# Attention into a gated FFN on one core: tile 1 in two token halves, and the last numerators of batch 1 moved back

## The chip, the core and the metric

The kernel runs on one NeuronCore of a Trainium2 chip. TensorE multiplies matrices and writes to PSUM, VectorE and ScalarE compute elementwise and read PSUM, GpSimd issues most transfers and converts some tiles, SyncE issues DMA transposes. Each engine works through its own instructions strictly in order, and waits for the others through semaphores. The metric is the device time of one execution in microseconds (us); it is given as the median of several executions.

## The reference

Linear attention with a positional weighting (cosine and sine of the position), for 8 batches of 8 heads, 576 positions and 64 features, and then a feed-forward network on the 4608 tokens:

```python
def phi(x, c, s):
    r = np.maximum(x, 0.0)
    return np.concatenate([r * c, r * s], axis=-1)      # 64 -> 128 features
q_p = phi(q, cos_w, sin_w)
k_p = phi(k, cos_w, sin_w)
kv  = np.einsum('bhsf,bhsd->bhfd', k_p, v)              # 128 x 64 for each head
z   = np.sum(k_p, axis=2)
num = np.einsum('bhsf,bhfd->bhsd', q_p, kv)
den = np.einsum('bhsf,bhf->bhs', q_p, z)[..., None] + 1e-06
attn = num / den
x = attn.transpose(0, 2, 1, 3).reshape(B * S, H * D)    # 4608 x 512
a = x @ w1; b = x @ w2                                  # 512 -> 1024
h = a * b @ w3                                          # 1024 -> 1024
out = h @ w_out                                         # 1024 -> 512
```

Nothing stands between w3 and w_out, so the kernel multiplies these two once (w34 = w3 @ w_out) and then uses one matrix of 1024 x 512.

## The kernel before

The positions of a batch are cut into five chunks (four of 128 and one of 64). A chunk is loaded, turned into features ("kp", "qp"; the cosine half on VectorE, the sine half on ScalarE), its key side is summed into KV, and its query side, transposed, is multiplied by KV: the numerator, with the denominator in a 65th column. VectorE normalizes it into "xblk", and a transpose of that becomes part of "xT", an FFN tile of 512 tokens. There are nine such tiles, t = 0 to 8. Batch b begins at token 576 b, so tile 1 (tokens 512 to 1023) holds the remainder of batch 0 (chunk 4) and of batch 1 its chunks 4, 0, 1 and 2, in this order; chunk 3 is already in tile 2.

The FFN is a generator that yields after every group of matmuls. Yields are numbered through all tiles, and slot g holds what attention work is emitted after group g:

```python
    g = 0
    for t in range(NT):
        for _ in ffn_groups(t):
            for u in slots[g]:
                u()
            g += 1
```

Tile 0 has the groups 0 to 39: 16 of products, then 16 that make w34 (two for each block of w3), then 8 of the second FFN matmul. Tile 1 has the groups 40 to 63: 16 of products (40 to 55) and 8 of the second matmul. So a slot number is a place in the order of every engine. In tiles 0 and 1 the first four column blocks (jc 0 to 3, as two pairs) are made for the first 256 tokens and then for the second, the other four at once for all 512:

```python
        def multiply(a, b, pair, half):
            asb = fsb.tile([P, 512], BF16, name="asb")
            nc.scalar.copy(out=asb[:], in_=a[:, :])
            nc.vector.tensor_mul(out=abT[:, ts(pair, 2), ts(half, 256)],
                                 in0=asb[:].rearrange("p (i n) -> p i n", i=2),
                                 in1=b[:, :].rearrange("p (i n) -> p i n", i=2))

        def on_half(half):
            # ... (tile 0's finer cut left out)
            for pair in range(2):
                a, b = ffn_tile(), ffn_tile()
                # ...
                    for ps, w in ((a, w1b), (b, w2b)):
                        for i in range(2):
                            products(ps[:, ts(i, 256)], w, 2 * pair + i, ts(half, 256))
                        if w is w1b and (t == 1 or half == 0):
                            yield
                multiply(a, b, pair, half)
                yield

        if t < 2:
            yield from on_half(0)
            yield from on_half(1)
        for jc in range(4 if t < 2 else 0, 8):
            aT = ffn_tile()
            products(aT[:, :], w1b, jc, slice(0, 512))
            asb = fsb.tile([P, 512], BF16, name="asb")
            nc.scalar.copy(out=asb[:], in_=aT[:, :])
            yield
            bT = ffn_tile()
            products(bT[:, :], w2b, jc, slice(0, 512))
            nc.vector.tensor_mul(out=abT[:, jc, :], in0=asb[:], in1=bT[:, :])
            yield
```

"ffn_tile" goes round four PSUM banks. "num" makes a numerator: for batches 0 and 1 into the one two-bank PSUM buffer "pnum", or, with in_two, into two FFN banks that are normalized one by one. The same "pnum" takes KV (line 305) of each batch. "no_more_by_pe" ends TensorE's transposes through PSUM, and opens a second buffer for numerators in their place.

```python
    def num(b, c, chain=True, in_two=False):
        # ...
        banks = [ffn_tile(), ffn_tile()] if in_two else [nt[:, g, :] for g in range(2)]
        for h in range(H):                                            # line 365
            nc.tensor.matmul(banks[h // 4][:, ds((h % 4) * 65, 65)], lhsT=qpT[:, h, ds(at, 128)],
                             rhs=kvs[:, h, :], start=True, stop=True)
        # ... then on VectorE, for the whole or for each half:
                nc.vector.tensor_scalar_add(out=den[rows, g], in0=n4[:, :, :, 64], scalar1=1e-6)
                nc.vector.reciprocal(out=den[rows, g], in_=den[rows, g])
                nc.vector.tensor_tensor(out=xblk[rows, g], in0=n4[:, :, :, 0:D], ...)   # line 383

    def x_tr(b, c, by_vector=False):
        # ... batches from 2 on, and two chunks of 0 and 1: by a DMA transpose
        for kc in range(4):                                           # line 417
            nc.tensor.transpose(pst[:, kc, :], xf[:, ts(kc, 128)], identb[:])
        copy = nc.vector.tensor_copy if by_vector else nc.scalar.copy
        copy(out=xT[t][:, :, ds(o, R)], in_=pst[:, 0:4, rows])        # line 419
```

A chunk of queries is transposed by TensorE ("q_tr", eight transposes and one evacuation by VectorE) or, where "dma_q" names it, by a DMA transpose right after its features.

Of the kernel before, what the change touches and what calls it, by code (L numbers as in the profile page):

```python
# [68 lines left out]
def kernel(  # L69
# [11 lines left out]
    nc = tc.nc  # L81
# [54 lines left out]
    def load_first4(eng, t, src, b=0):  # L136
        eng.dma_start(out=t[0:64, :, 4, :], in_=src[b, :, 512:S, :].rearrange("h p d -> p h d"))
# [9 lines left out]
    def load_w3(jp, n):  # L147
        nc.gpsimd.dma_start(out=w3b[:, jp:jp + n, :],
                            in_=moe_w3[ds(jp * P, n * P), :].rearrange("(b p) l -> p b l", p=P))

    def load_wout(half):
        nc.gpsimd.dma_start(out=woutb[:, ts(half, 4), :],
                            in_=moe_w_out[ts(half, 512), :].rearrange("(c p) m -> p c m", p=P))
# [44 lines left out]

    load_w12(0, 256)
    load_w12(256, 256)  # L200
    load_first4(nc.gpsimd, q0, q)
    nc.gpsimd.dma_start(out=w1b[:, :, ds(512, 256)], in_=w1v[:, :, ds(512, 256)])

    def other_loads(behind):

        seen = sm.tile([P, 1], BF16, name="seen", bufs=1)
        nc.gpsimd.tensor_copy(out=seen[:], in_=behind)
        nc.gpsimd.dma_start(out=w2b[:, :, ds(512, 256)], in_=w2v[:, :, ds(512, 256)])
        load_w12(768, 256)
        for jp in range(2):  # L210
            load_w3(jp, 1)
            load_wout(jp)
        for jp in range(2, 4):
            load_w3(jp, 1)
        load_w3(4, 2)
        load(1, "k")
        load_w3(6, 2)
# [25 lines left out]
    def order_of(b):  # L243

        return [0, 1, 2, 3, 4] if b % 2 == 0 else [4, 0, 1, 2, 3]

    def dma_q(b):

        return order_of(b)[5 if b < 1 else 3 if b == 1 else 0:]

    feat = {}

# [203 lines left out]
    def ffn_groups(t):  # L456
        x = xT[t]
        abT = fsb.tile([P, 8, 512], BF16, name="abT", bufs=2)

        def products(out, w, jc, tok):  # L460
            for kc in range(4):
                nc.tensor.matmul(out, lhsT=w[:, kc, ts(jc, 128)], rhs=x[:, kc, tok],  # L462
                                 start=(kc == 0), stop=(kc == 3))
# [10 lines that stand above are left out]
            if half == 1 and t == 0:  # L474
                banks = [(ffn_tile(), ffn_tile()) for _ in range(2)]
                for quarter in range(2):
                    for pair, (a, b) in enumerate(banks):
                        for i in range(2):
                            for ps, w in ((a, w1b), (b, w2b)):
                                products(ps[:, ds(256 * i + 128 * quarter, 128)], w, 2 * pair + i,  # L480
                                         ds(256 + 128 * quarter, 128))
                        if quarter == 1:
                            multiply(a, b, pair, half)
                        if quarter == 0 or pair == 1:
                            yield
                return
            for pair in range(2):
                a, b = ffn_tile(), ffn_tile()
                if pair == 0 and t == 0:
                    for quarter in range(2):  # L490
                        for i in range(2):
                            for ps, w in ((a, w1b), (b, w2b)):
                                products(ps[:, ds(256 * i + 128 * quarter, 128)], w, i,
                                         ds(256 * half + 128 * quarter, 128))
                            if half == 0 and quarter == 0 and i == 0:
                                yield
                        if quarter == 0:
                            yield
                else:
# [8 lines that stand above are left out]
        if t < 2:  # L508
            yield from on_half(0)
            yield from on_half(1)  # L510
        for jc in range(4 if t < 2 else 0, 8):
            aT = ffn_tile()
            products(aT[:, :], w1b, jc, slice(0, 512))
            asb = fsb.tile([P, 512], BF16, name="asb")
# [6 lines that stand above are left out]
        if t == 0:  # L521
            for jp in range(8):
                for part in range(2):
                    w34_mm(jp, part)
                    yield
            early.close()
            holds.append(ctx.enter_context(tc.tile_pool(name="hold", bufs=HELD,
                                                        reuse_waits="tile")))
        for ms in range(3 if t == NT - 1 else 4):
            ops = ffn_tile()  # L530
            for jc in range(8):
                nc.tensor.matmul(ops[:, :], lhsT=abT[:, jc, ts(ms, 128)], rhs=w34b[:, jc, :],  # L532
                                 start=(jc == 0), stop=(jc == 7))
                if jc == 3:
                    yield
            if ms % 2 == 0:
                osb = holds[0].tile([P, 2, 512], FP32, name="osb")
                kept.append(osb)
            nc.scalar.copy(out=osb[:, ms % 2, :], in_=ops[:, :])  # L539
            if t == NT - 1:  # L540
                store(nc.sync, osb[:, ms % 2:ms % 2 + 1, :], 4 * t + ms, 1)
            yield
        if t == NT - 1:
            for half in range(2):
                cols = ts(half, 256)
                ops = ffn_tile()
                for jc in range(8):
                    nc.tensor.matmul(ops[:, 0:256], lhsT=abT[:, jc, ts(3, 128)],  # L548
                                     rhs=w34b[:, jc, cols], start=(jc == 0), stop=(jc == 7))
                nc.scalar.copy(out=osb[:, 1, cols], in_=ops[:, 0:256])  # L550
                store(nc.sync, osb[:, 1:2, :], 4 * t + 3, 1, cols)
                yield
# [6 lines left out]
    def at(s, *calls):  # L559
        slots[s] += calls  # L560
# [8 lines left out]
    def plan(b, kf, vc, kv, qf, nu, loads=None, xt=None):  # L569
        order = order_of(b)  # L570
        for i, c in enumerate(order):
            at(kf[i], lambda c=c: prep_k(b, c))
            at(qf[i], lambda c=c: prep_q(b, c))
            at(vc[i], lambda c=c: prep_v(b, c))
        for i, c in enumerate(order):
            at(kv[i], lambda c=c, i=i: kv_chunk(b, c, i))
        for i, c in enumerate(order):
            at(nu[i], lambda c=c: num(b, c, in_two=b == 1 and c in (0, 2)))
            at(xt[i] if xt else nu[i], lambda c=c: x_tr(b, c, by_vector=(b, c) == (1, 1)))

    def plan_loads(b, when):
# [38 lines left out]
    at(1, lambda: x_tr(0, 1, by_vector=True), lambda: q_tr(0, 3, evac=False)[1](), lambda: num(0, 2))  # L620
    at(3, lambda: x_tr(0, 2), lambda: num(0, 3))
    at(5, lambda: x_tr(0, 3))
    at(6, lambda: features(0, q0f, q0, 4))
    at(23, lambda: transpose_q(0, 4))
    at(7, lambda: load(1, "qv"), lambda: load(2, "q"))
    at(29, lambda: num(0, 4))
    at(11, lambda: feature_buffers(1))
    at(29, lambda: x_tr(0, 4))

    for jp, s in enumerate((13, 16, 18, 20, 22, 24, 26, 28)):  # L630
        at(s, lambda jp=jp: w3_tr(jp))

    plan(1, kf=(24, 25, 26, 27, 28), vc=(31, 31, 32, 32, 32), kv=(33, 33, 33, 34, 34),
         qf=(29, 30, 30, 31, 31), nu=(35, 36, 38, 39, 42), xt=(37, 38, 40, 42, 42))
    for c, s in zip(order_of(1), (31, 32, 34)):
        at(s, lambda c=c: q_tr(1, c))
    at(43, no_more_by_pe)
    plan_loads(2, (27, 28, 33, 35))
    plan(2, kf=(36, 37, 38, 40, 41), vc=(41, 42, 43, 44, 45), kv=(46, 46, 46, 47, 47),
         qf=(40, 41, 42, 43, 44), nu=(48, 50, 52, 54, 57))  # L640
    plan_loads(3, (36, 37, 47, 50, 54, 57))
    plan(3, kf=(54, 57, 59, 61, 63), vc=(64, 65, 66, 67, 68), kv=(71, 72, 72, 73, 73),
# [54 lines left out]
```

## Time and profile before

| what | before |
|---|---|
| median of 3 executions | 249.2 us (249.05 to 250.78) |
| profiled span | 246.9 us, 5034 instructions |
| TensorE, VectorE, ScalarE, GpSimd busy | 97%, 55%, 53%, 38% |
| products with w1 and w2 (line 462), share of the chain that ended last | 45% |
| second FFN matmul (line 532), the same | 24% |
| DMA, the same | 10% |

The page calls the engines PE, DVE, ACT and POOL; SP is SyncE. A line of the timeline gives the start and the duration of an instruction (or of a run of the same, "x4"), both in us, the engine, the line of the kernel, the operation, and output and input by the names in the program; in brackets, the idle time before it and what ended this. A busy time is the sum of durations; instructions of one engine overlap a little, so the distance of two starts is the better pace. The chain that ended last follows the execution back from its last instruction, at each step to what released it.

### The profile page before, as it was taken

Reading aid. Unit: us, or ns where it says so; the run is one execution under the profiler, and the core shown is the slowest. Engines: PE = TensorE matmul, PEld = TensorE weight load, DVE = VectorE, ACT = ScalarE, POOL = GpSimd, SP = SyncE. Lnnn points to the kernel's source line nnn. Section 1 sums busy time; section 2 is a strip of 40 time slices with the busy share of each in tenths; the row PEclk is TensorE's granted clock in tenths of the full one; section 3 lists DMA queues with packets and bytes.
Section 4 is the critical chain, followed back from the end, with each engine's and each line's share of the span. In section 5 each row is a group of like instructions: output and inputs, shape, how many; then the busy total and the mean of one; then the engine's idle time right before and its main releaser. Section 6 shows DMA issues by size and latency. Waiting matters only on the chain.

```text
span 246.9 us, 5034 instructions
## 1 busy us (share of the span) xinstructions
PE 240.5 (97%) x1872; PEld 130.4 (53%) x1872; DVE 135.9 (55%) x336; ACT 130.2 (53%) x266; POOL 93.4 (38%) x196
## 2 busy tenths in 40 slices
PE   8799999999999999999999999999999999999994
PEld 3479545566975445444544555454545554444443
DVE  7775652668968445647566475547464645312420
ACT  2676313767943873466556654854575333434332
POOL 7654342024512261127032612173322005978700
PEclk9999999999999999999999999999999999999999
DMA  7999999999999969999999999999994536998823
GB/s 199 178 194 199 201 207 204 198 181 173 153 162 142 167 100 149 132 149 134 169 144 155 118 180 150 150 140 140 166 142 89 94 64 214 260 281 289 282 101 128
DMA packets 86200, 41.22 MB, mean 167 GB/s; under 512 B 53792, under 2 KB 82720, under 8 KB 86176
## 3 DMA queue, kind: packets, MB, share of 16 engines
q0 software_dynamic: 37008, 27.20, 71.8%
q1 hardware_dynamic: 49168, 13.71, 35.9%
q8 instruction: 14, 0.23, 0.4%
q14 instruction: 10, 0.08, 0.1%
HBM read 38.80 MB, written 9.44 MB: 195 GB/s over the span
## 4 chain that ended last, share of the span: by engine, by line
PE 85%; DMA 10%; POOL 3%; issue 1%; ACT 0%; POOLq 0%
PE ffnps L462 45%; PE ffnps L532 24%; PE ffnps L237 6%; DMA woutb<-in_moe_w_out_dram 5%; DMA w2b<-in_moe_w_dram 5%; PE pnum L365 4%; PE pnum L305 4%; PE pst L225 1%; PE ffnps L548 1%; POOL qs L133 1%; POOL w1b L196 1%; PE pst L336 1%; POOL vs L133 0%; PE pst L417 0%; POOL w2b L197 0%
## 5 line engine op out<-in xcount | busy, mean ns | idle before, releaser
L462 PE MATMUL ffnps<-xT,w2b 128*128 128x512 bf16 (+2 forms) x344 | 75.5, 344 | 0.0
L462 PE MATMUL ffnps<-xT,w1b 128*128 128x512 bf16 (+2 forms) x344 | 75.5, 344 | 0.0
L519 DVE TENSOR_TENSOR abT<-asb,ffnps 128x512 bf16<-128x512 bf16 x64 | 43.9, 686 | 54.3 <-PE ffnps L462 52.4
L532 PE MATMUL ffnps<-w34b,abT 128*128 128x512 bf16 x280 | 65.0, 379 | 0.0
L515 ACT CAST asb<-ffnps 128x512 bf16<-128x512 f32 x64 | 37.4, 584 | 50.0 <-PE ffnps L462 45.2
L462 PEld LDWEIGHTS <-w2b 128*128 128x128 bf16 x344 | 31.0, 98 | 27.3
L462 PEld LDWEIGHTS <-w1b 128*128 128x128 bf16 x344 | 30.8, 98 | 25.9
L567 POOL COPY seen<-mark 1x1 bf16<-1x1 bf16 x50 | 8.9, 178 | 84.4 <-ACT mark L565 84.4
L532 PEld LDWEIGHTS <-abT 128*128 128x128 bf16 x280 | 26.0, 98 | 27.9 <-DVE abT L519 0.2
L539 ACT COPY osb<-ffnps 128x512 f32<-128x512 f32 x35 | 20.5, 584 | 35.2 <-PE ffnps L532 35.1
L274 ACT ACTIVATE qp<-qs,sinv 128x512 bf16<-128x512 bf16 (+2 forms) x40 | 28.1, 714 | 1.8 <-DMA qs<-in_q_dram 1.8
L383 DVE TENSOR_TENSOR xblk<-pnum,den 128x512 bf16<-128x512 f32 (+1 forms) x37 | 25.6, 691 | 1.3
L297 POOL COPY va<-vs 128x512 bf16<-128x512 bf16 (+1 forms) x30 | 17.6, 621 | 22.9 <-DMA vs<-in_v_dram 22.4
L274 ACT ACTIVATE kp<-ks,sinv 128x512 bf16<-128x512 bf16 (+1 forms) x35 | 25.0, 717 | 0.9 <-DMA ks<-in_k_dram 0.9
L447 POOL DMA_DIRECT2D out_dram<-osb x42 | 22.1, 531 | 2.7 <-issue 2.1
L365 PEld LDWEIGHTS <-qpT 128*128 128x128 bf16 x320 | 15.4, 98 | 8.7 <-DVE qpT L350 0.6
L381 DVE TENSOR_SCALAR den<-pnum 128x8 f32<-128x8 f32 (+1 forms) x37 | 6.0, 163 | 22.6 <-PE pnum L365 22.5
L237 PE MATMUL ffnps<-woutb,w3T 128*128 128x512 bf16 x64 | 15.8, 380 | 0.2 <-DMA woutb<-in_moe_w_out_dram 0.2
L365 PE MATMUL pnum<-kvs,qpT 128*128 128x65 bf16 x296 | 15.8, 194 | 0.0
L270 DVE TENSOR_SCALAR qp<-qs,cosv 128x512 bf16<-128x512 bf16 (+1 forms) x40 | 15.3, 389 | 0.7 <-DMA qs<-in_q_dram 0.7
L305 PEld LDWEIGHTS <-kp 128*128 128x128 bf16 x280 | 11.4, 98 | 4.1
L270 DVE TENSOR_SCALAR kp<-ks,cosv 128x512 bf16<-128x512 bf16 (+1 forms) x35 | 12.5, 367 | 0.0
(88 smaller groups left out, 181.6 us busy)
## 6 DMA issues: line engine op xcount, KB each, us to landing
out_dram<-osb POOLq DMA_DIRECT2D x16, 256.0 KB, 4.5
out_dram<-osb POOLq DMA_DIRECT2D x24, 128.0 KB, 3.9
qs<-in_q_dram POOLq DMA_DIRECT2D x8, 256.0 KB, 7.6
ks<-in_k_dram POOLq DMA_DIRECT2D x6, 320.0 KB, 6.3
qs<-in_q_dram POOLq DMA_DIRECT2D x6, 320.0 KB, 5.9
vs<-in_v_dram POOLq DMA_DIRECT2D x6, 320.0 KB, 5.7
ks<-in_k_dram POOLq DMA_DIRECT2D x6, 256.0 KB, 7.0
vs<-in_v_dram POOLq DMA_DIRECT2D x6, 256.0 KB, 5.4
```

The costliest lines, as they stand in the source:

```text
L237: nc.tensor.matmul(acc[:, :], lhsT=w3T[:, lc, :], rhs=woutb[:, lc, :], start=(lc == 0), stop=(lc == 7))
L270: nc.vector.tensor_scalar(out=dst[:R, c, :, 0:D], in0=src[:R, :, c, :], scalar1=0.0, scalar2=cosv[:R, at:at + 1], op0=ALU.max, op1=ALU.mult)
L274: nc.scalar.activation(out=dst[:R, c, 0:n, D:F], in_=src[:R, 0:n, c, :], func=ACTF.Relu, scale=sinv[:R, at:at + 1], bias=0.0)
L305: nc.tensor.matmul(kvt[:, h // 4, ds((h % 4) * 65, 65)], lhsT=kp[:, c, h, :], rhs=va[:, c, h, 0:D + 1], start=(i == 0 and h % 4 == 0), sto ...
L365: nc.tensor.matmul(banks[h // 4][:, ds((h % 4) * 65, 65)], lhsT=qpT[:, h, ds(at, 128)], rhs=kvs[:, h, :], start=True, stop=True)
L383: nc.vector.tensor_tensor(out=xblk[rows, g], in0=n4[:, :, :, 0:D], in1=den[rows, g].unsqueeze(3).to_broadcast([R, G, 4, D]), op=ALU.mult)
L447: eng.dma_start(out=rows[:, :, cols], in_=osb[64 * i:64 * i + rows.shape[0], :, cols])
L462: nc.tensor.matmul(out, lhsT=w[:, kc, ts(jc, 128)], rhs=x[:, kc, tok], start=(kc == 0), stop=(kc == 3))
L515: nc.scalar.copy(out=asb[:], in_=aT[:, :])
L519: nc.vector.tensor_mul(out=abT[:, jc, :], in0=asb[:], in1=bT[:, :])
L532: nc.tensor.matmul(ops[:, :], lhsT=abT[:, jc, ts(ms, 128)], rhs=w34b[:, jc, :], start=(jc == 0), stop=(jc == 7))
L539: nc.scalar.copy(out=osb[:, ms % 2, :], in_=ops[:, :])
```

## The change

It is a change of order, with one piece of work moved to another engine:

- Tile 1 is made in two token halves over all eight column blocks, 8 groups of 256 tokens and then 8 more, so that its second half of tokens is first needed at group 48 and not at 44.
- This gives room for the numerators of batch 1's chunks 1, 2 and 3: from slots 38, 39 and 42 to 41, 43 and 45. Chunk 2's is no longer made in two FFN banks, and the end of TensorE's transposes through PSUM moves from slot 43 to 46. Batch 2's key features move from 36-41 to 38-42.
- A third chunk of batch 1's queries (chunk 1) is transposed by DMA instead of TensorE.
- Both halves of w_out are loaded before the second block of w3, and the first transposes of w3 stand one slot earlier.
- The remainder of batch 0's queries (chunk 4, 64 KB) is loaded behind that block and no longer before most weights; its features move from slot 6 to 19.

```diff
--- before.py
+++ after.py
@@ -198,7 +198,6 @@
 
     load_w12(0, 256)
     load_w12(256, 256)
-    load_first4(nc.gpsimd, q0, q)
     nc.gpsimd.dma_start(out=w1b[:, :, ds(512, 256)], in_=w1v[:, :, ds(512, 256)])
 
     def other_loads(behind):
@@ -207,9 +206,11 @@
         nc.gpsimd.tensor_copy(out=seen[:], in_=behind)
         nc.gpsimd.dma_start(out=w2b[:, :, ds(512, 256)], in_=w2v[:, :, ds(512, 256)])
         load_w12(768, 256)
-        for jp in range(2):
-            load_w3(jp, 1)
-            load_wout(jp)
+        load_w3(0, 1)
+        for half in range(2):
+            load_wout(half)
+        load_w3(1, 1)
+        load_first4(nc.gpsimd, q0, q)
         for jp in range(2, 4):
             load_w3(jp, 1)
         load_w3(4, 2)
@@ -246,7 +247,7 @@
 
     def dma_q(b):
 
-        return order_of(b)[5 if b < 1 else 3 if b == 1 else 0:]
+        return order_of(b)[5 if b < 1 else 2 if b == 1 else 0:]
 
     feat = {}
 
@@ -484,7 +485,7 @@
                         if quarter == 0 or pair == 1:
                             yield
                 return
-            for pair in range(2):
+            for pair in range(4 if t else 2):
                 a, b = ffn_tile(), ffn_tile()
                 if pair == 0 and t == 0:
                     for quarter in range(2):
@@ -508,7 +509,7 @@
         if t < 2:
             yield from on_half(0)
             yield from on_half(1)
-        for jc in range(4 if t < 2 else 0, 8):
+        for jc in range((4, 8)[t] if t < 2 else 0, 8):
             aT = ffn_tile()
             products(aT[:, :], w1b, jc, slice(0, 512))
             asb = fsb.tile([P, 512], BF16, name="asb")
@@ -575,7 +576,7 @@
         for i, c in enumerate(order):
             at(kv[i], lambda c=c, i=i: kv_chunk(b, c, i))
         for i, c in enumerate(order):
-            at(nu[i], lambda c=c: num(b, c, in_two=b == 1 and c in (0, 2)))
+            at(nu[i], lambda c=c: num(b, c, in_two=b == 1 and c == 0))
             at(xt[i] if xt else nu[i], lambda c=c: x_tr(b, c, by_vector=(b, c) == (1, 1)))
 
     def plan_loads(b, when):
@@ -620,23 +621,23 @@
     at(1, lambda: x_tr(0, 1, by_vector=True), lambda: q_tr(0, 3, evac=False)[1](), lambda: num(0, 2))
     at(3, lambda: x_tr(0, 2), lambda: num(0, 3))
     at(5, lambda: x_tr(0, 3))
-    at(6, lambda: features(0, q0f, q0, 4))
+    at(19, lambda: features(0, q0f, q0, 4))
     at(23, lambda: transpose_q(0, 4))
     at(7, lambda: load(1, "qv"), lambda: load(2, "q"))
     at(29, lambda: num(0, 4))
     at(11, lambda: feature_buffers(1))
     at(29, lambda: x_tr(0, 4))
 
-    for jp, s in enumerate((13, 16, 18, 20, 22, 24, 26, 28)):
+    for jp, s in enumerate((12, 16, 18, 20, 22, 24, 26, 28)):
         at(s, lambda jp=jp: w3_tr(jp))
 
     plan(1, kf=(24, 25, 26, 27, 28), vc=(31, 31, 32, 32, 32), kv=(33, 33, 33, 34, 34),
-         qf=(29, 30, 30, 31, 31), nu=(35, 36, 38, 39, 42), xt=(37, 38, 40, 42, 42))
-    for c, s in zip(order_of(1), (31, 32, 34)):
+         qf=(29, 30, 30, 31, 31), nu=(35, 36, 41, 43, 45), xt=(37, 38, 43, 45, 45))
+    for c, s in zip(order_of(1), (31, 32)):
         at(s, lambda c=c: q_tr(1, c))
-    at(43, no_more_by_pe)
+    at(46, no_more_by_pe)
     plan_loads(2, (27, 28, 33, 35))
-    plan(2, kf=(36, 37, 38, 40, 41), vc=(41, 42, 43, 44, 45), kv=(46, 46, 46, 47, 47),
+    plan(2, kf=(38, 39, 40, 41, 42), vc=(41, 42, 43, 44, 45), kv=(46, 46, 46, 47, 47),
          qf=(40, 41, 42, 43, 44), nu=(48, 50, 52, 54, 57))
     plan_loads(3, (36, 37, 47, 50, 54, 57))
     plan(3, kf=(54, 57, 59, 61, 63), vc=(64, 65, 66, 67, 68), kv=(71, 72, 72, 73, 73),
```

## The prediction

> **What bounds the kernel now.** First the page's busy table, the chain that ended last, and the table of stretches.
>
> ```profile
> PE 240.5 (97%) x1872; PEld 130.4 (53%) x1872; DVE 135.9 (55%) x336; ACT 130.2 (53%) x266; POOL 93.4 (38%) x196
> ...
> PE 85%; DMA 10%; POOL 3%; issue 1%; ACT 0%; POOLq 0%
> ```
>
> ```profile
> 34.00:50.00 16.00, 15.98 (x115) 8.22 (x115) 7.01 (x16) 8.15 (x16) 4.34 (x8) 1.00 1.30 202
> 50.00:62.00 12.00, 12.00 (x144) 7.79 (x143) 9.00 (x31) 8.29 (x20) 3.99 (x10) 1.00 1.33 175
> 62.00:79.00 17.00, 17.00 (x184) 12.26 (x182) 14.08 (x37) 10.46 (x22) 5.25 (x12) 1.00 1.19 150
> ```
>
> TensorE (the first number after the comma) is busy without a gap through the stages that the change touches. So there is almost no wait to remove: 10% of the chain is DMA, but only because the chain is followed back from one wait of 0.18 us, at 34.02 us, for the second w_out block. What can be won is TensorE work; what can be lost is a new wait. The last stretch is the thin one: VectorE (third column) is busy 14.08 of 17.00 us.
>
> Then the timelines of 57 to 68 us, where tile 0 ends and tile 1 begins. ScalarE, then TensorE, then VectorE:
>
> ```profile
> 60.42 0.57 ACT L419 COPY xT<-pst 128x512 bf16<-128x512 bf16 x1
> 60.90 0.72 ACT L274 ACTIVATE kp<-ks,sinv 128x512 bf16<-128x512 bf16 x1
> 61.52 0.56 ACT L539 COPY osb<-ffnps 128x512 f32<-128x512 f32 x1
> 61.98 0.72 ACT L274 ACTIVATE qp<-qs,sinv 128x512 bf16<-128x512 bf16 x1
> 62.61 0.71 ACT L274 ACTIVATE kp<-ks,sinv 128x512 bf16<-128x512 bf16 x1
> 63.22 0.56 ACT L467 CAST asb<-ffnps 128x512 bf16<-128x512 f32 x1
> ```
>
> ```profile
> 59.85 0.39 PE L417 MATMUL pst<-identb,xblk 128*128 128x128 bf16 x4
> 60.08 0.42 PE L365 MATMUL pnum<-kvs,qpT 128*128 128x65 bf16 x8
> 60.34 1.02 PE L532 MATMUL ffnps<-w34b,abT 128*128 128x512 bf16 x4
> ...
> 62.33 0.39 PE L417 MATMUL pst<-identb,xblk 128*128 128x128 bf16 x4
> 62.55 1.04 PE L462 MATMUL ffnps<-xT,w2b 128*128 128x256 bf16 x8
> ```
>
> ```profile
> 60.97 0.69 DVE L383 TENSOR_TENSOR xblk<-pnum,den 128x512 bf16<-128x512 f32 x1
> ...
> 64.56 0.67 DVE L468 TENSOR_TENSOR abT<-asb,ffnps 128x512 bf16<-128x512 bf16 x1
> ```
>
> See three things. Starts give the real pace: a feature ACTIVATE lasts 0.72 us but the next instruction starts 0.62 later; a copy out of PSUM takes a 0.48 pace. ScalarE has no gap here, and the first asb of tile 1, whose product was ready at 62.5, comes at 63.22. And chunk 1 of batch 1 is normalized (60.97) before VectorE reaches the first multiply of tile 1 (64.56), so its transposes at 62.33 find it ready.
>
> **What the Trainium skill says.** "TensorE: Matmul & The Clock Gate", section "Back-to-back issue gap", gives 262 cycles for 256 columns and 518 for 512: two half matmuls cost one whole. The trace agrees: eight of 256 columns take 0.87 us (61.46 to 62.33), four of 512 take 0.86 (60.34 to 61.20). "Perfetto Trace Analysis", section "Optimizing Scalar/DVE Operations", says that a profiled latency overlaps the next instruction; hence 0.62 against 0.72. The same section says that engines which aren't saturated can still cause bubbles on others; here ScalarE is 53% busy overall and full from 59 to 68 us. "DMA: Bandwidth & Descriptors", section "Issuing engines are not separate DMA queues": transfers of all issuers share 16 engines, so moving a transpose to a DMA isn't free; the trace has 2.7 to 7.6 us to landing for the transposes issued between 50 and 70 us.
>
> **The change part by part.**
>
> *Tile 1 in two halves over all columns.* 32 matmuls of 512 columns become 64 of 256: by the durations above 8 x 0.87 against 8 x 0.86, +0.1 us at most. Evacuations stay at 8 casts and 8 multiplies. The second token half is now needed at group 48 instead of 44; that is what lets the numerators move.
>
> *Third query chunk by DMA.* Takes away 8 transposes, 0.45 us of TensorE (55.22 to 55.66), and one 0.68 us evacuation on VectorE. That brings the numerator of chunk 4 forward to 56.08, but its second four heads need the KV copy of VectorE, which ends at 56.25 (55.82 + 0.43) and does not move: 0.09 back. Chunk 1's features are ready at about 51; the DMA has until 62 to land. Net -0.36.
>
> *w_out ahead of the second w3 block.* When a queue is full, the issue timeline of GpSimd gives the landings:
>
> ```profile
> 26.86 0.68 POOL L127 DMA_DIRECT2D ks<-in_k_dram  x1 [0.57 <-DMA w3b<-in_moe_w_dram]
> 30.51 0.71 POOL L148 DMA_DIRECT2D w3b<-in_moe_w_dram  x1 [2.97 <-DMA woutb<-in_moe_w_out_dram]
> 31.51 0.69 POOL L123 DMA_DIRECT2D qs<-in_q_dram  x1 [0.29 <-DMA w3b<-in_moe_w_dram]
> 34.26 0.68 POOL L127 DMA_DIRECT2D qs<-in_q_dram  x1 [2.06 <-DMA woutb<-in_moe_w_out_dram]
> ```
>
> Landings: w3 block 0 about 26.8, w_out half 0 30.5, w3 block 1 31.5, w_out half 1 about 34.0. In the new order w_out half 1 lands about 1.0 earlier and w3 block 1 last. The small query load no longer stands before them, about 0.4 (my reading of 1.7 us between two landings that are otherwise 1.3 apart), so w3 block 1 lands near 33.6. TensorE reaches its transposes at about 33.2, after the first half product, waits 0.4, does 0.45 and starts the second half product at 34.05, against 34.02. Zero: the wait changes its name.
>
> *The query remainder (chunk 4 of batch 0) later.* Its features go from slot 6 to 19, so its DMA transpose starts at about 38.5 instead of 23.68. Before, this transpose took 9.2 us. Landing then is 47.7, and its numerator starts at 48.41: it fits by 0.7, with no certainty. I put 0.2 us for it.
>
> *The later numerators of batch 1.* Nothing is removed: merging chunk 2's two small normalizations saves VectorE about 0.45. But the order in its queue turns round. Chunk 1's numerator is now in slot 41, after the first multiply of tile 1, and five k features move from slots 36-41 to 38-42, on top of five q features in 40-44. By hand, with the paces above and my start times:
>
> 1. Transposes of chunk 0 at 59.50 (59.85, less 0.36, rounded). ScalarE copies them at 59.93 (0.43 after their start, as elsewhere in the trace).
> 2. Before the first asb ScalarE has: that copy 0.48, k feature 0.62, osb 0.48, k 0.62, q 0.62, k 0.62, in all 3.44. So asb starts at 63.37 and ends at 63.93, though its product was ready at 61.6.
> 3. VectorE waits for it: multiply 63.96 (pace 0.61), then den, reciprocal and product of chunk 1 (0.20 + 0.24 + 0.69): 65.70.
> 4. TensorE has from 59.50 on 0.22 + 4 x 0.865 (groups 39 to 42) + 0.26 (numerator) + 0.87 (group 43) = 4.8, and reaches chunk 1's transposes in slot 43 at 64.32. They can start at 65.76. Wait 1.44.
> 5. Two transposes' worth later the same again: asb 1 starts after four more features (63.37 + 0.48 + 4 x 0.62 = 66.33, ends 66.89), multiply 66.93 to 67.54, evacuation of chunk 1's transposes 0.34, normalization of chunk 2 from 67.88 to 69.01. TensorE is at chunk 2's transposes at 67.98. Wait 1.1.
> 6. Numerator of chunk 3 in slot 45 (done 69.6), group 46 to 70.42, then batch 2's KV in slot 46, which needs the same PSUM buffer. VectorE has two q features and multiply 2 (to 70.14), then chunk 3's normalization to 71.27. Wait 0.9.
>
> Sum: 1.44 + 1.1 + 0.9 - 0.36 + 0.1 + 0.2 = +3.4. Counted as start of group 48, which does the same work in both kernels: 73.5 against 70.42, +3.05 without the last two terms. Behind it TensorE is dense to the end, so nothing gives this back. Small terms are as likely to vanish as not: I take +2.8, from 249.2 to 252.0.
>
> **The rivals.**
> A: no new wait, only the TensorE work falls. For it: the kernel before hides a 0.7 us late asb behind four PSUM banks, and the change was plainly meant to give slack. Against: step 4 doesn't rest on the banks but on VectorE's order, numerator behind multiply. It would give 249.2 - 0.4 = 248.8.
> B: the late query remainder becomes the wait. For: 202 GB/s and full DMA slices from 34 to 50 us. Against: other transposes landed in 2.7 to 7.6. With 11 us instead of 9.2 it costs 1.1 more: 253.1 on top of my waits, 249.9 alone.
> C: w3 block 1 lands later than 33.6 since both w_out halves stand before it; up to 1 us, 253 with the rest.
> D: the removed wait was worth more than its 0.18. Against: the chain shows nothing else between 34 and 62 us that isn't TensorE; at most 0.3 us.
>
> **Range and chances.** About 0.75 for the three waits in some size (their sum between 2 and 4), 0.25 for rival A or near it. That gives 248.9 to 253.8 for 8 in 10. 2% is 5.0 us: faster would need 244.2, more than anything on offer, 0.01; slower needs 254.2, the waits together with B and C, 0.06; within 2% 0.93.
>
> **What would show it.** In the profile after: TensorE waits at the transposes of batch 1 (line 417 of before) for VectorE's xblk at about 64.3 and 68, and the KV matmuls wait near 70.4; the first asb of tile 1 starts 1.5 us or more after its product; TensorE's transposes of queries are 8 fewer; the wait at 34 names w3 instead of w_out. I am wrong if TensorE is busy throughout 59 to 72 us, or if its largest gap is at the last numerator of batch 0 near 48 us.

## The result, and the profile after

252.4 us median (251.9 to 252.9) against 249.2, with 252.0 predicted: ratio 1.0113, 95% interval [1.0074, 1.0152]. The profiled span went from 246.9 to 250.2 us. The table of stretches of the changed kernel (stretch, its length, then busy time of TensorE, its weight loads, VectorE, ScalarE and GpSimd):

```profile
34.00:50.00 16.00, 16.00 (x121) 8.34 (x121) 7.56 (x18) 9.63 (x18) 4.11 (x8) 1.00 1.33 198
50.00:62.00 12.00, 11.94 (x134) 7.80 (x132) 6.52 (x24) 7.43 (x18) 3.35 (x8) 1.00 1.46 165
62.00:79.00 17.00, 13.68 (x183) 11.87 (x181) 12.09 (x31) 9.37 (x20) 4.65 (x9) 1.00 1.24 153
```

The work that TensorE loses is in the last stretch: it is busy for 13.68 of 17.00 us, where it was 17.00. The timeline names the places. TensorE, at the waits:

```profile
62.74 1.04 PE L463 MATMUL ffnps<-xT,w2b 128*128 128x256 bf16 x8
65.01 0.40 PE L418 MATMUL pst<-identb,xblk 128*128 128x128 bf16 x4 [1.23 <-DVE xblk L384]
...
68.26 0.40 PE L418 MATMUL pst<-identb,xblk 128*128 128x128 bf16 x4 [0.85 <-DVE xblk L384]
...
71.02 0.93 PE L306 MATMUL pnum<-va,kp 128*128 128x65 bf16 x24 [1.24 <-DVE xblk L384]
```

The brackets count from the modelled end of the matmul before. From start to start (65.01 less 62.74, less the 0.87 that eight such matmuls take elsewhere) the three gaps are 1.40, 1.02 and 1.40 us. All further gaps are counted so. Behind them, ScalarE and VectorE of the changed kernel:

```profile
61.39 0.72 ACT L275 ACTIVATE qp<-qs,sinv 128x512 bf16<-128x512 bf16 x1
62.00 0.71 ACT L275 ACTIVATE kp<-ks,sinv 128x512 bf16<-128x512 bf16 x1
62.62 0.57 ACT L468 CAST asb<-ffnps 128x512 bf16<-128x512 f32 x1
```

```profile
63.22 0.69 DVE L469 TENSOR_TENSOR abT<-asb,ffnps 128x512 bf16<-128x512 bf16 x1 [3.67 <-ACT asb L468]
63.83 0.16 DVE L382 TENSOR_SCALAR den<-pnum 128x8 f32<-128x8 f32 x1
64.02 0.20 DVE L383 RECIPROCAL den<-den 128x8 f32<-128x8 f32 x1
64.26 0.69 DVE L384 TENSOR_TENSOR xblk<-pnum,den 128x512 bf16<-128x512 f32 x1
```

VectorE stands idle for 3.67 us before the multiply, though chunk 1's numerator was done at about 62 (its matmuls start at 61.61): the queue is in order, and the multiply in front waits for a cast that stands behind features. The normalization ends at 64.95, and 0.06 later TensorE goes on.

The ledger of the two profiled executions, by starts: first product of tile 0 0.53 earlier (15.52 against 16.05), no wait at w34's second half product -0.34, eight transposes fewer -0.45, the KV wait behind them +0.23, the three gaps +3.82, and 0.44 more between the last matmul and the end. Sum 3.2, measured 3.3. The first two terms, 0.87 together, are taken up in experiment 3: the start is chance, and the wait at 34 us varies.

### The profile page after: what moved, and what is told of

It reads as the page before. It is cut to its first block, busy times and chain, and to the rows that moved or that the text cites. A ratio compares the mean times of both kernels' runs of the same rounds, so it can differ in the third digit from the quotient of the medians.

```text
span 250.2 us, 5083 instructions
## 1 busy us (share of the span) xinstructions
PE 241.5 (97%) x1896; PEld 133.0 (53%) x1896; DVE 135.2 (54%) x332; ACT 130.4 (52%) x266; POOL 93.7 (37%) x196
## 4 chain that ended last, share of the span: by engine, by line
PE 92%; ACT 3%; DVE 3%; issue 1%; ACTq 0%
PE ffnps L463 47%; PE ffnps L533 23%; PE ffnps L238 6%; PE pnum L366 4%; PE unread L186 4%; PE pnum L306 4%; PE pst L226 1%; ACT kp L275 1%; ACT qp L275 1%; PE pst L337 1%; PE ffnps L549 1%; PE pst L418 1%; DVE xblk L384 1%; DVE abT L469 1%; DVE qp L271 0%
## 5 line engine op out<-in xcount | busy, mean ns | idle before, releaser
L520 DVE TENSOR_TENSOR abT<-asb,ffnps 128x512 bf16<-128x512 bf16 x60 | 41.2, 686 | 53.1 <-PE ffnps L463 52.6
L516 ACT CAST asb<-ffnps 128x512 bf16<-128x512 f32 x60 | 35.0, 584 | 45.4 <-PE ffnps L463 43.5
L463 PEld LDWEIGHTS <-w2b 128*128 128x128 bf16 x360 | 32.6, 98 | 26.4
L463 PEld LDWEIGHTS <-w1b 128*128 128x128 bf16 x360 | 32.2, 98 | 25.0
L384 DVE TENSOR_TENSOR xblk<-pnum,den 128x512 bf16<-128x512 f32 (+1 forms) x38 | 26.3, 691 | 1.4
L271 DVE TENSOR_SCALAR qp<-qs,cosv 128x512 bf16<-128x512 bf16 (+1 forms) x40 | 16.1, 409 | 0.6 <-DMA qs<-in_q_dram 0.6
L306 PE MATMUL pnum<-va,kp 128*128 128x65 bf16 x280 | 12.0, 193 | 1.2 <-DVE xblk L384 1.2
```

The lines of the kernel that those rows point to most:

```text
L306: nc.tensor.matmul(kvt[:, h // 4, ds((h % 4) * 65, 65)], lhsT=kp[:, c, h, :], rhs=va[:, c, h, 0:D + 1], start=(i == 0 and h % 4 == 0), sto ...
```

## The experiments

Each edit is against the kernel before or the changed one, as named. "Gaps" are TensorE's, from start to start. Some lines of the edits are cut off at their end where nothing changes, and further changes are named in a comment (#).

**1. Numerators one slot earlier** (changed kernel):

```diff
-         nu=(35, 36, 41, 43, 45), xt=(37, 38, 43, 45, 45))
+         nu=(35, 36, 40, 42, 44), xt=(37, 38, 43, 45, 45))
```

> Edit: the changed kernel, with the numerators of batch 1's chunks 1, 2 and 3 one slot earlier (40, 42, 44 instead of 41, 43, 45), so that each stands ahead of a multiply in VectorE's queue and not behind it; all else as changed. Queue theory (TensorE waits because the normalizations stand on VectorE behind a multiply that waits for a late asb): the TensorE gaps at the transposes of chunks 1 and 2 and at batch 2's KV, 1.40 + 1.02 + 1.40 us from start to start, all but vanish; 252.4 becomes 248.3 to 249.5. Rival (ScalarE is simply overfull in tile 1, or the halves or the third DMA transpose are what TensorE waits for): moving by one slot takes away at most a third of the 3.8, so 251 or more.

250.44 us, ratio to before 1.0063 [1.0043, 1.0083]. The first gap is gone, 0.66 and 0.97 are left: 1.6 of 3.8. The order in VectorE's queue is a cause, but my number missed. Chunk 2's normalization still stands behind the multiply of the pair before, which waits 0.38 for its late asb; chunk 3's stands behind features that take 0.44 and 0.69 instead of 0.34 (experiments 8 and 9).

**2. Numerators back, the rest as changed:** slots, two banks for chunk 2, key features and the end of TensorE's transposes as before.

```diff
-         nu=(35, 36, 41, 43, 45), xt=(37, 38, 43, 45, 45))
+         nu=(35, 36, 38, 39, 42), xt=(37, 38, 40, 42, 42))
-    plan(2, kf=(38, 39, 40, 41, 42),
+    plan(2, kf=(36, 37, 38, 40, 41),
# and in_two for chunks 0 and 2; no_more_by_pe at 43
```

> Edit: the changed kernel with the numerators, their transposes, chunk 2 in two banks, batch 2's key features and the end of TensorE's transposes all back at the slots of before; the halves over all columns, the third DMA transpose and the order of loads stay. Queue theory: no TensorE gap of over 0.2 us between 57 and 72 us, and the rest of the change shows its worth: about 1.1 us under the kernel before, 247.6 to 248.6. Rival (halves or DMA transpose cost something themselves): gaps stay in this stretch and the time stays above 249.2.

250.23 us, 1.0047 [1.0022, 1.0072]. No gap between 57 and 72 us, so the three waits belong to the moved numerators and features. But the rest of the change isn't worth 1.1 us; it costs. A wait for a DMA has come up behind the stage:

```profile
75.98 1.04 PE L463 MATMUL ffnps<-xT,w1b 128*128 128x256 bf16 x8
77.82 0.43 PE L366 MATMUL pnum<-kvs,qpT 128*128 128x65 bf16 x8 [0.80 <-DMA qpT<-qp]
```

TensorE stands there until the queries of a chunk of batch 2, transposed by DMA, have landed.

**3. The loads alone** (kernel before, with the four load edits of the change):

```diff
-    load_first4(nc.gpsimd, q0, q)
+        load_w3(0, 1); load_wout(0); load_wout(1); load_w3(1, 1); load_first4(nc.gpsimd, q0, q)
-    at(6, lambda: features(0, q0f, q0, 4))
+    at(19, lambda: features(0, q0f, q0, 4))
-    for jp, s in enumerate((13, 16, 18,
+    for jp, s in enumerate((12, 16, 18,
# the five loads stand one to a line; the old loop over load_w3(jp, 1) and load_wout(jp) goes
```

> Edit: the kernel before with the loads alone changed: w_out ahead of the second w3 block, the query remainder loaded and worked on later, w3's first transposes a slot earlier. If the 0.95 us by which the changed kernel is ahead at 33 us come from these loads: 248.0 to 248.5, no wait at the second half product of w34. If 0.5 of them (ahead already at 12 us) are chance between two executions: 248.7 to 248.9. My prediction on record had 0 for it: 249.2.

249.00 us against 248.91, 0.9993 [0.9973, 1.0013]: nothing that shows in the median. The lead of 0.5 us at the first product was chance between two executions: this run starts it at 15.81, and so does experiment 4, which has the old loads. The wait at 34 us varies: in the five profiles with the old order of loads it is 0.34 (before), 0.23, 0.18 and twice none, and none of the nine with the new order has it. So the new order takes away a small wait that is not always there, and the prediction's zero holds within the noise of 0.2%.

**4. Halves and moved numerators, no loads, no DMA** (kernel before, with the halves, the slots of the changed kernel and chunk 2 in one buffer):

```diff
-            for pair in range(2):
+            for pair in range(4 if t else 2):
-         nu=(35, 36, 38, 39, 42), xt=(37, 38, 40, 42, 42))
+         nu=(35, 36, 41, 43, 45), xt=(37, 38, 43, 45, 45))
-    plan(2, kf=(36, 37, 38, 40, 41),
+    plan(2, kf=(38, 39, 40, 41, 42),
# and jc from 8 for tile 1, in_two for chunk 0 alone, no_more_by_pe at 46
```

> Edit: the kernel before with tile 1 in two halves over all columns and the later numerators and key features alone; loads and query transposes as before. Queue theory: the whole loss and none of the gain, three gaps of about 1.4, 1.0 and 1.4 us; 249.2 + 3.8 = 253, 252.4 to 253.6. Rival (the third DMA transpose or the later loads are part of the waits): under 252.

251.95 us, 1.0123 [1.0093, 1.0153]. Gaps 1.40, 1.02 and 0.87. These edits alone give a loss that can't be told from that of the whole change (1.0113). The third gap is 0.53 smaller than in the changed kernel, and the time under my range for it.

**5. Halves alone** (kernel before):

```diff
-            for pair in range(2):
+            for pair in range(4 if t else 2):
-        for jc in range(4 if t < 2 else 0, 8):
+        for jc in range((4, 8)[t] if t < 2 else 0, 8):
```

> Edit: the kernel before with tile 1 in two token halves over all columns, and nothing else. By the durations 0.1 us more TensorE work: 248.8 to 249.3, no gap between 60 and 72 us. Rival (half groups with the cast bound to the multiply starve the four banks): gaps at the products of tile 1, over 249.6.

248.69 against 248.81 us, 0.9999 [0.9985, 1.0013], no gap between 60 and 72 us. Twice as many matmuls of half the width cost nothing that shows here.

**6. The third DMA transpose alone** (kernel before):

```diff
-        return order_of(b)[5 if b < 1 else 3 if b == 1 else 0:]
+        return order_of(b)[5 if b < 1 else 2 if b == 1 else 0:]
-    for c, s in zip(order_of(1), (31, 32, 34)):
+    for c, s in zip(order_of(1), (31, 32)):
```

> Edit: the kernel before with the third query chunk of batch 1 transposed by DMA, and nothing else. My prediction's step: 0.45 us of TensorE less and 0.09 to 0.23 of KV wait, 248.5 to 248.8. Rival, from the run with the numerators back, which had a wait of 0.96 us for a later query transpose of batch 2 near 78 us and 0.48 us more behind the last store: the added transfer pushes batch 2's transposes back, 249.5 to 250.3.

249.91 against 248.81 us, 1.0038 [1.0022, 1.0054]: it costs about 1 us (1.1 between the medians) where my step gave it a gain. TensorE:

```profile
59.62 1.02 PE L532 MATMUL ffnps<-w34b,abT 128*128 128x512 bf16 x4
61.26 0.43 PE L365 MATMUL ffnps<-kvs,qpT 128*128 128x65 bf16 x8 [0.61 <-DMA qpT<-qp]
```

The numerator of chunk 2, whose queries went by DMA before too, now waits 0.78: the new transpose takes 8.2 us to land and the two behind it, of chunks 2 and 3, take 8.6 and 8.8, where the kernel before had 6.2 and 7.9. 0.21 more are lost at 77.65, before a numerator of batch 2 whose transposed queries land at 77.60. And batch 2's v comes later; GpSimd converts it in these lines, of before and of this run:

```profile
62.72 2.94 POOL L297 COPY va<-vs 128x512 bf16<-128x512 bf16 x5 [0.52 <-PE pst L417]
```

```profile
65.78 3.00 POOL L297 COPY va<-vs 128x512 bf16<-128x512 bf16 x5 [4.30 <-DMA vs<-in_v_dram]
```

Three us later, and so in every run that has the third transpose (65.1 to 66.8), and in none of those without (61.9 to 62.7). The last 0.44 us are in experiment 10.

**7. The cast ahead of the features** (changed kernel):

```diff
                         for i in range(2):
                             products(ps[:, ts(i, 256)], w, 2 * pair + i, ts(half, 256))
+                        if w is w1b and t == 1:
+                            asb = cast(a)
                         if w is w1b and (t == 1 or half == 0):
                             yield
-                multiply(a, b, pair, half)
+                multiply(a, b, pair, half, asb)
# cast(a) is the first two lines of multiply, which makes asb itself only where none is given
```

> Edit: the changed kernel, where in tile 1 ScalarE's cast (asb) is emitted right behind the w1 products, ahead of the slot's features, and not one slot later with the multiply; numerators stay at 41, 43, 45. Queue theory: the first asb starts 1.2 us (two features) earlier, near 61.4, the multiply no longer waits for it, and the first gap of 1.39 us shrinks to under 0.3; the second asb is 1.2 us earlier too, but TensorE arrives 1.4 us earlier at the second gap, so 0.6 to 1.2 us stay there and as much at KV. Sum 1.2 to 2.5 instead of 3.8: 250.0 to 251.2. Rival (it is only the place behind the multiply in VectorE's queue, whatever ScalarE does): gap one keeps over 1 us, 252 or more.

251.56 us, 1.0107 [1.0080, 1.0133]. Gap one falls to 0.18, as the queue theory has it: ScalarE's features are the other half of the cause. The sum, 2.8, is over my range. The second gap stays at 1.02, since asb and TensorE both come about as much earlier; the third grows to 1.60, for a reason that the trace shows and that is taken up with the third wait below.

The other way to relieve ScalarE, **batch 2's key features back to 36 to 41** (changed kernel):

```diff
-    plan(2, kf=(38, 39, 40, 41, 42),
+    plan(2, kf=(36, 37, 38, 40, 41),
```

> Edit: the changed kernel with batch 2's key features at the slots of before (36, 37, 38, 40, 41) and all else as changed. Queue theory: ScalarE has two features less before the first asb, so it starts 1.2 us earlier; gap one shrinks from 1.39 to under 0.4, the two others stay, as with the early cast; 250.8 to 251.8. Rival (the key features' place doesn't matter, the waits are the numerators' alone): 252 or more.

252.09 us, 1.0100 [1.0062, 1.0138]; gaps 0.80, 1.23, 0.87. Less than I expected: ScalarE had idle time before chunk 0's copy, and only about one feature really leaves the stretch between this copy and the first cast.

**8. Early cast and even slots together**, first with the third DMA transpose (the edits of 1 and 7), then with TensorE in its place (and the edit of 6 undone):

> Edit: both at once, the early cast and the numerators at slots 40, 42 and 44; all else as changed. Queue theory: no gap over 0.3 us is left between 60 and 70 us; the sum under 0.6. What is then left over the kernel before is what the third DMA transpose costs elsewhere: 249.0 to 250.2. If gaps of over 0.6 us stay, something other than the two queues keeps TensorE waiting.

249.73 us, 1.0038 [1.0024, 1.0052]; gaps of 0.29 and 0.76 are left. By the sign I had set, the gap of 0.76 means that something besides the two queues is at work: the feature ahead of chunk 3's normalization takes 0.70 us here, with GpSimd's copies of v running from 65.91, and those before the copies take 0.34 or 0.35.

> Edit: the changed kernel with the early cast and the even slots, and the third query chunk of batch 1 transposed by TensorE again, as before. Theory (what is left of the loss, 0.9 us, is the third DMA transpose: it delays batch 2's v load by 3 us, so GpSimd's copies of it meet VectorE's normalization of chunk 3, and it moves the last store's semaphore to the front of the final list of waits): v lands by 63 us, the KV gap shrinks from 0.76 to under 0.3, nothing but 0.06 us of waits behind the last store; 248.4 to 249.1, the same as the kernel before. Rival (the leftover is the crowd on VectorE in tile 1, with or without the transfer): the KV gap stays over 0.6 and the time over 249.2.

250.24 us, 1.0040 [1.0027, 1.0054]: a miss. v is there earlier, and yet there is a gap of 1.28 before chunk 3's numerator (and 0.52 at KV). GpSimd and VectorE of this run:

```profile
62.51 2.95 POOL L298 COPY va<-vs 128x512 bf16<-128x512 bf16 x5 [1.27 <-DMA vs<-in_v_dram]
```

```profile
63.03 0.78 DVE L271 TENSOR_SCALAR qp<-qs,cosv 128x512 bf16<-128x512 bf16 x1
63.74 0.69 DVE L271 TENSOR_SCALAR kp<-ks,cosv 128x512 bf16<-128x512 bf16 x1
64.35 0.67 DVE L473 TENSOR_TENSOR abT<-asb,ffnps 128x512 bf16<-128x512 bf16 x1
64.95 0.65 DVE L271 TENSOR_SCALAR qp<-qs,cosv 128x512 bf16<-128x512 bf16 x1
65.52 0.34 DVE L271 TENSOR_SCALAR kp<-ks,cosv 128x512 bf16<-128x512 bf16 x1
```

As long as GpSimd copies (to 65.46) a feature on VectorE takes 0.65 to 0.78 us, and 0.34 after it. Chunk 2's normalization, behind three such features, ends 1 us later than with the third DMA transpose, counted from chunk 1's.

**9. The copies taken away from GpSimd** (last kernel of 8):

```diff
-        eng = nc.vector if b < 2 else nc.gpsimd
+        eng = nc.vector if b < 3 else nc.gpsimd
-    plan(2, kf=(38, 39, 40, 41, 42), vc=(41, 42, 43, 44, 45),
+    plan(2, kf=(38, 39, 40, 41, 42), vc=(44, 45, 45, 46, 46),
```

> Edit: as in the run before with the early cast, the even slots and the query chunk by TensorE, and now batch 2's five conversions of v on VectorE (slots 44 to 46) instead of GpSimd, so that GpSimd has nothing to do between 61 and 70 us. If GpSimd's copies are what slows VectorE's features down (0.65 to 0.78 us each beside them, 0.34 without), the features of slots 40 to 42 take 0.35 each, chunk 2 is normalized 1 us earlier and the gap of 1.28 us before chunk 3's numerator falls under 0.4; the KV gap (0.52) may grow, since up to three conversions of 0.25 now stand ahead of it: 248.9 to 250.0. If the features stay over 0.6 us and the gap over 1, it isn't GpSimd.

250.06 us, 1.0040 [1.0020, 1.0060]. The features take 0.34 and 0.35, and the gap of 1.28 is 0.18: it was GpSimd. The time doesn't fall, since KV now waits for the conversions themselves, 0.63 + 0.79, more than I had allowed.

**10. One SyncE transfer more** (kernel before):

```diff
-    load_first4(nc.sync, k0, k)
+    nc.sync.dma_start(out=k0[0:64, 0:4, 4, :], in_=k[0, 0:4, 512:S, :].rearrange("h p d -> p h d"))
+    nc.sync.dma_start(out=k0[0:64, 4:8, 4, :], in_=k[0, 4:8, 512:S, :].rearrange("h p d -> p h d"))
```

> Edit: the kernel before, with SyncE's small load of the last key chunk of batch 0 split in two by heads, so that SyncE has issued one transfer more when the last store comes; nothing else. If the 0.44 us behind the last store come only from which semaphore of SyncE's round the last store gets: the last store's semaphore becomes 108, which SyncE's final list awaits second instead of ninth, seven more waits of 0.06 us follow the landing; 249.1 to 249.5 against 248.8, and the time from the last matmul to the end is 3.89 instead of 3.45 us. Rival (those 0.44 belong to the transposes in flight or to chance): 248.6 to 249.0 and 3.45.

250.04 against 249.11 us, 1.0029 [1.0013, 1.0045]. From the start of the last matmul to the end it is 3.9 us instead of 3.45, as in the kernels with the third DMA transpose. SyncE's last waits in the trace, us of start and semaphores, before and here:

```
before          244.54 106,105 ... 245.36 117,107   245.99 118,109   (last store: 118, landed 245.97)
one_more_dma    245.45 106,105     246.91 108,104   246.97 112,103 ... 247.34 118,109   (last store: 108, landed 246.89)
```

In these traces SyncE's transfers go round a set of semaphores, and the end awaits these in one order, 0.06 us each. If the last store has the last of them, nothing follows; if it has the second, seven more waits do. The end is as expected, but the time is over my range. In the profiled execution the rest is two waits, of 0.31 and 0.89 us, for transposes of xT at 132 and 180 us; that they explain the other executions too is not shown. Such a wait near 180 us comes and goes (0.39 to 0.89 in five of the runs, none in the kernel before or the changed one); I did not find what decides it.

No version beat the kernel before. But for the wait at 34 us TensorE is dense in it from 18 us on, so work that is moved on other engines can at best stay hidden.

## Why the prediction was right, point by point

- **TensorE bounds it, no wait worth removing: right.** Halves alone and loads alone change nothing that shows (5 and 3).
- **Three new waits: right, with the mechanism.** Predicted 1.44, 1.1 and 0.9; measured 1.40, 1.02 and 1.40. Moving the numerator ahead of the multiply (1) or the cast ahead of the features (7) each takes the first away. Steps 1 to 4 hold to 0.05 us once the 0.7 us are taken off by which the changed kernel's execution ran ahead of my times: asb at 62.62 for 63.37, the normalization's end at 64.95 for 65.70, TensorE's arrival at 63.61 for 64.32. They only add up starts in two queues.
- **The third wait: mis-sized by 0.5.** The term was "two q features and multiply 2 (to 70.14)", with 0.52 for the two features. They took 1.05 to the start of the multiply: GpSimd's copies of v started 4 us later (66.78, against 62.45 in experiment 4) and fell upon them. GpSimd and VectorE of the changed kernel, then VectorE of experiment 4, where the copies ended at 65.27:

```profile
66.78 2.94 POOL L298 COPY va<-vs 128x512 bf16<-128x512 bf16 x5 [6.34 <-DMA vs<-in_v_dram]
68.12 1.12 DVE L271 TENSOR_SCALAR qp<-qs,cosv 128x512 bf16<-128x512 bf16 x2
69.17 0.67 DVE L469 TENSOR_TENSOR abT<-asb,ffnps 128x512 bf16<-128x512 bf16 x1
```

```profile
68.72 0.60 DVE L270 TENSOR_SCALAR qp<-qs,cosv 128x512 bf16<-128x512 bf16 x2
69.24 0.67 DVE L468 TENSOR_TENSOR abT<-asb,ffnps 128x512 bf16<-128x512 bf16 x1
```

  Four traces agree on it. With the features at 0.52 the gap is 0.87 (experiment 4, and the key features back, where v lands late too but the copies end at 68.07, before these features); with 1.05 it is 1.40 (the changed kernel), with 1.25 it is 1.60 (the early cast).
- **"Net -0.36" for the third query chunk: wrong.** The 0.45 and the KV wait (0.23 instead of 0.09) are there; the wait is longer because the whole numerator of chunk 4, and not only its second four heads, starts behind VectorE's KV copy (copy to 55.40, numerator at 55.45). But alone the move costs about 1 us (6): later transposes land late, v lands late, the end gets 0.44 longer. I had asked only whether its own landing was in time (it was, at 59.2), and my "2.7 to 7.6 us to landing" left out a 7.9. In the changed kernel the three gaps hide the two waits for late transposes, but neither the longer end nor the longer third gap. That the working's sum of +3.4 still came near the measured 3.2 is in part luck: gaps, KV wait and end less the eight transposes make +4.0 in the profiled execution, and the early start and the missing wait at 34 us took 0.87 off.
- **w_out order zero: right in size, wrong in its reason.** I predicted that the wait at 34 us would take the name of w3; TensorE has no wait there at all with the new order (3). w3's second block landed by 32, not 33.6:

```profile
30.83 0.71 POOL L148 DMA_DIRECT2D w3b<-in_moe_w_dram  x1 [1.87 <-DMA woutb<-in_moe_w_out_dram]
32.04 0.69 POOL L123 DMA_DIRECT2D qs<-in_q_dram  x1 [0.50 <-DMA w3b<-in_moe_w_dram]
```

- **The query remainder fits: right.** Its transpose was issued at 37.63 and landed 7.6 us later, at 45.2, before its numerator at 47.55.
- **Rival A** (no new wait) fell with the three gaps, **B** (the remainder) and **C** (w3) with the two points above, **D** (the removed wait worth more) with experiment 3.

## What to carry to other kernels

Slack is a matter of queues: an instruction given more slots until its result is needed can still become late, if its new place is behind one that waits for another engine's backlog. Before moving work, write down for each in-order queue what stands between the data and the consumer, with the trace's own start-to-start paces; here that gave 3.4 us for three waits that measured 3.8. And a transfer that is in time itself still has to be charged for those behind it.

## What the runs showed of the hardware

- VectorE's bf16 features (SBUF to SBUF) take 0.34 us alone and mostly 0.65 to 0.78 beside GpSimd's copies of 0.6 us (23 of the 31 that start among these copies in all runs; the other 8 take 0.33 to 0.59); products with a PSUM operand stay at 0.67 to 0.69. This is what the Trainium skill has in "SBUF — State Buffer", section "Who interferes with whom": VectorE's second port pair is GpSimd's, and one blocks the other. Experiment 9 and 23 of the 31 agree with it.
- One DMA transpose of 128 x 1024 bf16 more (1056 packets by the page's queue table) made a v load land 3 us later and the two transposes behind it take 8.6 and 8.8 us instead of 6.2 and 7.9 (experiment 6). For 0.45 us of TensorE that was a bad trade here.
- Which semaphore the last store gets was worth 0.44 us here (experiment 10).
